# Another order for the first phase of a chunked attention and Mish feed-forward kernel

## The chip, the cores and the metric

The kernel runs on one core of a Trainium2 chip. The metric is the time of one execution on the device in microseconds (us); smaller is better. A core has five engines that run side by side and wait for each other through semaphores: TensorE (PE in the profile; PEld is its weight load), VectorE (DVE), ScalarE (ACT), GpSimd (POOL) and SyncE (SP, which here only issues DMA transfers). Each engine takes its instructions in the order in which they were written.

## The reference

Attention inside chunks of 64 tokens, then a feed-forward layer with Mish on its output:

```
scores = q_c @ k_c.T / sqrt(64)            # per batch, head and chunk of 64 tokens
attn = exp(scores - max); attn = attn / (sum(attn) + 1e-9)
x = (attn @ v_c)  -> 4608 tokens x 512
h = x @ w_in                               # 512 x 2048
g = h * tanh(softplus(h))                  # Mish
out = g @ w_out                            # 2048 x 512
```

All inputs are 32-bit floats, but for the two weights, which the kernel reads as pairs of 32-bit words and turns into 32-bit floats itself.

## The kernel before, in words

**Precision.** Each operand of the two large products is kept as a high part (rounded to the type of the fast matmul) and a low part (the rest). A product is three matmuls: low by high, high by high, high by low. `up` (line 282) does this for h = x W_in, 12 matmuls for a tile of 128 features and 512 tokens; `down` (L328) for the output.

**Weights.** There are 32 weight tiles of 128 x 512, 16 of W_in (i0 to i15) and 16 of W_out (o0 to o15), taken in the order i0, i1, i2, o0, i3, o1, i4, ... A tile goes through five steps. `load` (L82): one DMA of 512 KB. `scale` (L87): two ACT passes, L91 for the upper words (into a tile `wic` or `woc`) and L100 for the lower words (in place, in `wis` or `wos`; for i0 and i1 one byte each). `bits` (L105): two DVE passes, a shift (L110 or L113) and a merge with the sign (L114). `hi` (L121): an ACT copy into `wi_h` or `wo_h`. `lo` (L124): a DVE subtraction into `wi_l` or `wo_l`. All of it is done once, in the first ninth of the tokens' work.

**Attention.** Tokens come in pairs of 128-token tiles: 18 pairs, two to a block of 512 tokens. The steps of a pair are scores (PE, `s`), max and subtraction (DVE, `m`, `p`), exponential (ACT L220), sum, reciprocal and norm (DVE), transposes (PE, `pt`), a copy (ACT L251, `ps`), values (PE, `av`) and the split of x into `xh` (ACT L272) and `xl` (DVE L275).

**The first phase.** `prologue` (L383) does pairs 0 and 1, each as two halves (FIRST and SECOND, one tile each), between the first steps of the weight tiles i0, i1, i2, o0 and i3. `keep_busy` (L369) puts matmuls between that nobody reads (`spare`). The first `up`, on the columns A of pair 0, stands ahead of the transposes of pair 1, and the one on the columns B of pair 1 behind its values. After that come the slots (L452): in each, one `up`, one `down`, and the steps of two weight tiles as long as there are any.

**What sets the order.** Everything is written out by hand under `manual_schedule`: the order of the calls is the order of each engine's instructions. The pool of the raw weight tiles has four buffers, so a `load` waits on SP until the steps of an earlier tile are done. A new table of functions is loaded on ACT where the kind of function changes (`ACT_TABLE_LOAD`); the one at L417 is drawn by an activation of one column, `early`.

Of the kernel before, what the change touches and what calls it, by code (L numbers as in the profile page):

```python
# [18 lines left out]
P = 128  # L19
# [5 lines left out]
def kernel(  # L25
# [58 lines left out]
        nc.sync.dma_start(out=a.rearrange("p n t -> p (n t)"), in_=w32[m][f])  # L84
        wc[m, f] = {"a": a}

    def w_scale(m, f):  # L87
        d = wc[m, f]
        a = d["a"]
        d["c"] = c = wst.tile([P, DM], U32, name=f"w{m}c_{f}", tag="c")  # L90
        nc.scalar.activation(  # L91
            out=c.bitcast(F32), in_=a[:, :, 1].bitcast(F32), func=AF.Copy, scale=2.0**-112
        )
        low = a[:, :, 0]
        if bytewise(m, f):
            out = a.rearrange("p n t -> p (n t)").bitcast(U8)
            out = out.rearrange("p (n b) -> p n b", b=8)[:, :, 4]
        else:
            out = low.bitcast(I32)
        nc.scalar.activation(out=out, in_=low, func=AF.Copy, scale=7.499 / 2.0**32)  # L100

    def bytewise(m, f):
        return m == "i" and f < 2

    def w_bits(m, f):  # L105
        c, a = wc[m, f]["c"], wc[m, f]["a"]
        left, both, either = ALU.logical_shift_left, ALU.bitwise_and, ALU.bitwise_or
        sign = 0x80000000
        if bytewise(m, f):
            nc.vector.tensor_scalar(out=c, in0=c, scalar1=3, scalar2=None, op0=left)  # L110
            sign |= 7
        else:
            nc.vector.scalar_tensor_tensor(out=c, in0=c, scalar=3, in1=a[:, :, 0], op0=left, op1=either)  # L113
        nc.vector.scalar_tensor_tensor(out=c, in0=a[:, :, 1], scalar=sign, in1=c, op0=both, op1=either)  # L114

    def w_dst(m, f, part):
        if m == "o":
# [15 lines left out]
    for f in range(NF):  # L133
        order += [("i", f + 2)] if f + 2 < NF else []
        order += [("o", f)]
    steps = {"load": w_load, "scale": w_scale, "bits": w_bits, "hi": w_hi, "lo": w_lo}

    def w(step, n):
        if n < len(order):
            steps[step](*order[n])  # L140
# [143 lines left out]
    it = {}  # L284
    acc = {}

    def up(i, cols=slice(0, TOK), last="x"):

        b, f = divmod(i, NF)
        xh, xl = xts[b]  # L290
        if i not in it:
            it[i] = {"h": ps_h.tile([P, TOK], F32, name=f"h_{i}", tag="h")}
        h = it[i]["h"]
        n = 0
        parts = ((wi_l, xh), (wi_h, xh), (wi_h, xl))
        for w_, x in parts if last == "x" else reversed(parts):
            for kt in range(NK):
                nc.tensor.matmul(  # L298
                    h[:, cols],
                    lhsT=w_[:, f, kt],  # L300
                    rhs=x[:, kt, cols],
                    start=(n == 0),
                    stop=(n == 3 * NK - 1),
                )
                n += 1

    def mish(i):
        d = it[i]
# [66 lines left out]
    def prologue():  # L375

        A, B = slice(0, PTOK), slice(PTOK, TOK)
        O0, O2 = (ps_o, "o0"), (ps_o, "o2")
        room = xp.tile([P, 2, 2, H, CHUNK], F32, name="room_qk", tag="xh")
        room_v = xp.tile([P, 2, 2, H, CHUNK], F32, name="room_v", tag="xl")  # L380
        load_qk(0, None, (FIRST, SECOND), (nc.sync, nc.scalar))
        w("load", 0)
        load_v(0, room_v[:, 0])  # L383
        load_qk(1, (room[:, 0], room[:, 1]), (FIRST, SECOND))
        w("load", 1)
        load_v(1, room_v[:, 1])
        w("load", 2)
        w("load", 3)
        for t, place in (FIRST, HOME), (SECOND, O0):
            keep_busy(7 if t == FIRST else 3)  # L390
            a_scores(0, t, place)
            a_max(0, t)
            a_sub(0, t)
            a_exp(0, t)
        w("scale", 0)
        for t, place in (FIRST, O2), (SECOND, HOME):
            a_inverse(0, t)
            a_norm(0, t)
            keep_busy(9 if t == FIRST else 3)
            a_transpose(0, t, place)  # L400
            a_copy(0, t)
        w("bits", 0)
        w("hi", 0)
        w("lo", 0)
        for t, place in (FIRST, O0), (SECOND, O2):
            a_values(0, t, place)
        for t in FIRST, SECOND:
            a_hi(0, t)
            a_lo(0, t)
        w("scale", 1)  # L410
        for t, place in (FIRST, HOME), (SECOND, O0):
            a_scores(1, t, place)
            a_max(1, t)
            a_sub(1, t)
            a_exp(1, t)
        w("scale", 2)
        nc.scalar.activation(out=early, in_=ident[:, :1], func=AF.Mish)  # L417
        load_qk(2)
        w("load", 4)
        up(0, A)  # L420
        for t, place in (FIRST, O2), (SECOND, HOME):
            a_inverse(1, t)
            a_norm(1, t)
            keep_busy(8 if t == FIRST else 4)
            a_transpose(1, t, place)
            a_copy(1, t)
        w("bits", 1)
        w("hi", 1)
        w("bits", 2)
        for t, place in (FIRST, O0), (SECOND, O2):  # L430
            a_values(1, t, place)
        for t in FIRST, SECOND:
            a_hi(1, t)
            a_lo(1, t)
        w("hi", 2)
        w("scale", 3)
        w("load", 5)
        w("lo", 1)
        w("lo", 2)
        w("bits", 3)  # L440
        w("scale", 4)
        up(0, B)
        up(1, last="w")
        mish(0)
        w("load", 6)

# [10 lines left out]
    def slot(s):  # L457
        a = plan.get(s, {})
        n = 2 * s + 3

        if 1 <= s and s + 1 < N:
            up(s + 1, last="w")
        if "t" in a:
            a_transpose(a["t"])
        if "v" in a:
            a_values(a["v"])
        if "s" in a:
            a_scores(a["s"])
        if 1 <= s <= N:
            down(s - 1)  # L470

        w("load", n + 4)
        w("hi", n)
        if s < N:
            g_hi(s)
            g_lo(s)
        w("scale", n + 2)
        w("bits", n + 1)
        w("lo", n)
        if "max" in a:  # L480
            a_max(a["max"])
        if "norm" in a:
            a_norm(a["norm"])
        if "t" in a:
            a_copy(a["t"])
        if "exp" in a:
# [73 lines left out]
```

## Time and profile before

| | |
|---|---|
| Time, median of 3 runs | 877.64 us (875.27 to 877.67) |
| The profiled execution's own time | 876.71 us |
| Its span, first to last instruction | 874.9 us |
| PE busy | 860.4 us, 98% of the span |
| DVE busy | 341.5 us, 39% |
| ACT busy | 256.0 us, 29% |
| DMA queue of the transfers (q1) | 53.49 MB, 20.5% of 16 engines' span |

The span is cut into what each engine did. A share of busy time is a mean over the whole span: in the second to the fifth fortieth of it (22 to 109 us) the page shows DVE and ACT at 80% or more, while the weights are made, and both at 10 to 50% afterwards; PE is at 90% or more from the second fortieth to the last but one. The last instruction ends at 874.9 us; the run's own time is 1.8 us more.

### The profile page before, as it was taken

Reading aid. Unit: us, or ns where it says so; the run is one execution under the profiler, and the core shown is the slowest. Engines: PE = TensorE matmul, PEld = TensorE weight load, DVE = VectorE, ACT = ScalarE, POOL = GpSimd, SP = SyncE. Lnnn points to the kernel's source line nnn. Section 1 sums busy time; section 2 is a strip of 40 time slices with the busy share of each in tenths; the row PEclk is TensorE's granted clock in tenths of the full one; section 3 lists DMA queues with packets and bytes.
Section 4 is the critical chain, followed back from the end, with each engine's and each line's share of the span. In section 5 each row is a group of like instructions: output and inputs, shape, how many; then the busy total and the mean of one; then the engine's idle time right before and its main releaser. Section 6 shows DMA issues by size and latency. Waiting matters only on the chain.

```text
span 874.9 us, 13635 instructions
## 1 busy us (share of the span) xinstructions
PE 860.4 (98%) x5984; PEld 709.6 (81%) x5984; DVE 341.5 (39%) x533; ACT 256.0 (29%) x362; POOL 0.7 (0%) x6
## 2 busy tenths in 40 slices
PE   7999999999999999999999999999999999999997
PEld 6877788888888888888888888888888888888886
DVE  5889854242433233333424242423342342422221
ACT  5888832121312112221212131212212121311111
POOL 0000000000000000000000000000000000000000
PEclk9999999999999999999999999999999999999999
DMA  7557512101310130102110131013011202002001
GB/s 289 195 167 245 189 37 61 49 25 49 73 49 25 49 73 25 49 26 51 46 55 18 50 73 49 25 50 73 25 49 49 50 23 73 1 1 49 1 0 49
DMA packets 25179, 55.40 MB, mean 63 GB/s; under 512 B 2592, under 2 KB 2592, under 8 KB 25120
## 3 DMA queue, kind: packets, MB, share of 16 engines
q1 hardware_dynamic: 24512, 53.49, 20.5%
q8 instruction: 47, 0.77, 0.4%
q10 hardware_dynamic: 608, 1.05, 0.3%
q14 instruction: 12, 0.10, 0.0%
HBM read 45.09 MB, written 9.44 MB: 62 GB/s over the span
## 4 chain that ended last, share of the span: by engine, by line
PE 91%; DVE 4%; ACT 3%; issue 2%; ACTq 0%; POOLq 0%; POOL 0%
PE o_o L340 41%; PE h L298 41%; PE s L170 2%; PE av L170 2%; PE pt L241 2%; PE o_a L340 1%; PE spare L371 1%; DVE wo_l L125 1%; DVE wic L113 1%; DVE woc L114 1%; DVE wi_l L125 1%; DVE woc L113 0%; DVE m L197 0%; DVE xl L275 0%; ACT L310 0%
## 5 line engine op out<-in xcount | busy, mean ns | idle before, releaser
L318 DVE CAST gh<-z 128x512 fp32r<-128x512 f32 x136 | 57.8, 425 | 468.2 <-PE o_o L340 468.2
L340 PE MATMUL o_o<-wo_h,gl 128*128 128x512 f32 x560 | 222.9, 398 | 0.3 <-DVE gl L323 0.3
L340 PE MATMUL o_o<-wo_l,gh 128*128 128x512 f32 x560 | 218.4, 390 | 1.4 <-DVE wo_l L125 1.4
L340 PE MATMUL o_o<-wo_h,gh 128*128 128x512 f32 x560 | 218.3, 390 | 0.0
L310 ACT ACTIVATE z<-h 128x512 f32<-128x512 f32 x144 | 86.2, 599 | 450.7 <-PE h L298 344.7
L298 PE MATMUL h<-xh,wi_l 128*128 128x512 f32 (+1 forms) x580 | 154.9, 389 | 0.8 <-ACT xh L272 0.8
L298 PE MATMUL h<-xh,wi_h 128*128 128x512 f32 (+1 forms) x580 | 154.6, 388 | 0.0
L298 PE MATMUL h<-xl,wi_h 128*128 128x512 f32 (+1 forms) x580 | 154.6, 389 | 0.0
L298 PEld LDWEIGHTS h<-xh,wi_l 128*128 128x128 f32 x580 | 108.8, 189 | 23.3 <-ACT xh L272 0.9
L298 PEld LDWEIGHTS h<-xh,wi_h 128*128 128x128 f32 x580 | 108.9, 189 | 22.3
L298 PEld LDWEIGHTS h<-xl,wi_h 128*128 128x128 f32 x580 | 108.7, 189 | 22.2
L340 PEld LDWEIGHTS o_o<-wo_h,gl 128*128 128x128 f32 x560 | 105.1, 188 | 23.5 <-ACT z L310 0.7
L340 PEld LDWEIGHTS o_o<-wo_l,gh 128*128 128x128 f32 x560 | 105.2, 188 | 22.2 <-DVE wo_l L125 1.7
L340 PEld LDWEIGHTS o_o<-wo_h,gh 128*128 128x128 f32 x560 | 105.1, 188 | 22.1
L323 DVE TENSOR_TENSOR gl<-z,gh 128x512 fp32r<-128x512 f32 x144 | 99.7, 692 | 8.3 <-ACT gh L316 3.6
L251 ACT COPY ps<-pt 128x1024 f32<-128x1024 f32 (+1 forms) x20 | 18.6, 932 | 81.8 <-PE pt L241 81.8
L310 ACT ACT_TABLE_LOAD x16 | 20.5, 1283 | 34.5 <-PE h L298 34.5
L354 DVE COPY ob<-o_o 128x512 f32<-128x512 f32 x17 | 11.8, 692 | 35.2 <-ACT ob L356 32.8
L197 DVE TENSOR_REDUCE m<-s 128x16 f32<-128x1024 f32 (+1 forms) x20 | 22.2, 1112 | 7.5 <-PE s L170 7.4
L170 PEld LDWEIGHTS s<-k,q 64*64 64x64 f32 x1088 | 17.7, 135 | 6.4 <-issue 5.5
L211 DVE TENSOR_TENSOR p<-s,m 128x1024 f32<-128x1024 f32 (+1 forms) x20 | 22.3, 1117 | 0.6
L275 DVE TENSOR_TENSOR xl<-av,xh 128x1024 fp32r<-128x1024 f32 (+1 forms) x20 | 22.1, 1111 | 0.9 <-ACT xh L272 0.9
(48 smaller groups left out, 407.3 us busy)
## 6 DMA issues: line engine op xcount, KB each, us to landing
out<-ob SPq DMA_DIRECT2D x68, 128.0 KB, 2.4
wis<-in_w_in SPq DMA_DIRECT2D x16, 512.0 KB, 3.5
wos<-in_w_out SPq DMA_DIRECT2D x16, 512.0 KB, 3.8
q<-in_q SPq DMA_DIRECT2D x16, 512.0 KB, 3.7
k<-in_k SPq DMA_DIRECT2D x16, 512.0 KB, 3.7
v<-in_v SPq DMA_DIRECT2D x16, 512.0 KB, 4.0
room_v<-in_v SPq DMA_DIRECT2D x2, 512.0 KB, 7.3
q<-in_q SPq DMA_DIRECT2D x2, 256.0 KB, 3.9
```

Of the source, the lines that this page charges most:

```text
L125: nc.vector.tensor_tensor(out=w_dst(m, f, 1), in0=wc.pop((m, f))["c"].bitcast(F32), in1=w_dst(m, f, 0).bitcast(F32), op=ALU.subtract,)
L170: nc.tensor.matmul(o[h * CHUNK : (h + 1) * CHUNK, c, t - ts.start, g], lhsT=l[rows, t, 2 * g + h], rhs=r[rows, t, 2 * g + h], start=True, ...
L197: nc.vector.tensor_reduce(out=small(j, "m", t), in_=st[j]["s", t.start].rearrange("p c t g k -> p c (t g) k"), op=ALU.max, axis=AX.X,)
L211: nc.vector.tensor_tensor(out=d["p"][:, t].rearrange("p t g c k -> p c (t g) k"), in0=d["s", t.start].rearrange("p c t g k -> p c (t g) k" ...
L241: nc.tensor.transpose(out=d["pt", ts.start][:, t - ts.start, g], in_=d["p"][:, t, g].rearrange("p c k -> p (c k)"), identity=ident,)
L251: nc.scalar.copy(out=d["ps"][:, t].rearrange("p t h k -> p (t h k)"), in_=d["pt", t.start][:, : t.stop - t.start].rearrange("p t g n -> p ...
L275: nc.vector.tensor_tensor(out=x_view(j, 1, t), in0=flat(st[j]["av", t.start]), in1=x_view(j, 0, t).bitcast(F32), op=ALU.subtract,)
L298: nc.tensor.matmul(h[:, cols], lhsT=w_[:, f, kt], rhs=x[:, kt, cols], start=(n == 0), stop=(n == 3 * NK - 1),)
L310: nc.scalar.activation(out=d["z"], in_=d["h"], func=AF.Mish)
L318: nc.vector.tensor_copy(out=d["gh"], in_=d["z"])
L323: nc.vector.tensor_tensor(out=d["gl"], in0=d["z"], in1=d["gh"].bitcast(F32), op=ALU.subtract)
L340: nc.tensor.matmul(acc[t], lhsT=g[:, sl], rhs=w_[:, f], start=(f == 0 and n == 0), stop=(f == NF - 1 and n == 2),)
```

## The change

No arithmetic is changed, and no instruction added or taken away: every engine has as many rows as before. Four steps of the weights can now be called apart (`w_upper` and `w_lower` for `w_scale`, `w_shift` and `w_merge` for `w_bits`), and `prologue` calls them elsewhere. `up` takes its three groups of four matmuls by number: 0 is low x by high weights, 1 is high by high, 2 is high x by low weights.

```
-        w("hi", 0)
-        w("lo", 0)
+        w("shift", 1)
         for t, place in (FIRST, O0), (SECOND, O2):
             a_values(0, t, place)
         for t in FIRST, SECOND:
             a_hi(0, t)
             a_lo(0, t)
-        w("scale", 1)
+        w("hi", 0)
+        w("lower", 1)
...
-        w("scale", 2)
         nc.scalar.activation(out=early, in_=ident[:, :1], func=AF.Mish)
         load_qk(2)
-        w("load", 4)
-        up(0, A)
+        up(0, A, (0, 1))
...
             a_copy(1, t)
-        w("bits", 1)
-        w("hi", 1)
-        w("bits", 2)
+            if t == FIRST:
+                w("scale", 2)
+        w("lo", 0)
+        w("merge", 1)
+        w("load", 4)
+        w("shift", 2)
         for t, place in (FIRST, O0), (SECOND, O2):
             a_values(1, t, place)
         for t in FIRST, SECOND:
             a_hi(1, t)
             a_lo(1, t)
+        w("hi", 1)
+        w("merge", 2)
         w("hi", 2)
         w("scale", 3)
...
-        up(0, B)
-        up(1, last="w")
+        up(0, A, (2,))
+        up(0, B, (1, 2, 0), (1, 2, 0))
+        up(1)
         mish(0)
```

Besides, `w("upper", 1)` stands behind the copy of pair 0's first half. The slots keep their order.

First place: ACT, from the copies of pair 0's transposes (`ps<-pt`) to the exponentials of pair 1. `wic_170` is the scaled tile of i0, `wis_109` the raw tile of i1, `av` the values. Before:

```order
L251 COPY ps_192<-pt_0_187 128x512
L251 COPY ps_192<-pt_1_202 128x512
L122 CAST wi_h<-wic_170 128x512
L272 CAST xh_246<-av_0_212 128x2x4x64
L272 CAST xh_246<-av_1_229 128x2x4x64
L91 ACTIVATE wic_252<-wis_109 128x512
L100 ACTIVATE wis_109<-wis_109 128x512
L220 ACTIVATE p_274<-p_274 128x512 x2
```

After:

```order
L265 COPY ps_192<-pt_0_187 128x512
L90 ACTIVATE wic_194<-wis_109 128x512
L265 COPY ps_192<-pt_1_204 128x512
L286 CAST xh_247<-av_0_213 128x2x4x64
L286 CAST xh_247<-av_1_230 128x2x4x64
L135 CAST wi_h<-wic_170 128x512
L102 ACTIVATE wis_109<-wis_109 128x512
L234 ACTIVATE p_274<-p_274 128x512 x2
```

The upper words of i1 are scaled between the two copies, the two `xh` come ahead of the copy `wi_h` of i0, and the lower words of i1 stay behind them.

Second place: ACT, from the exponentials of pair 1 to the copy of i2 (`wis_112` raw, `wic_298` or `wic_332` scaled). Before:

```order
L91 ACTIVATE wic_298<-wis_112 128x512
L100 ACTIVATE wis_112<-wis_112 128x512
L417 ACT_TABLE_LOAD
L417 ACTIVATE early<-ident 128x1
L251 COPY ps_339<-pt_0_334 128x512
L251 COPY ps_339<-pt_1_350 128x512
L122 CAST wi_h<-wic_252 128x512
L272 CAST xh_246<-av_0_361 128x2x4x64
L272 CAST xh_246<-av_1_378 128x2x4x64
L122 CAST wi_h<-wic_298 128x512
```

After:

```order
L431 ACT_TABLE_LOAD
L431 ACTIVATE early<-ident 128x1
L265 COPY ps_330<-pt_0_325 128x512
L90 ACTIVATE wic_332<-wis_112 128x512
L102 ACTIVATE wis_112<-wis_112 128x512
L265 COPY ps_330<-pt_1_344 128x512
L286 CAST xh_247<-av_0_355 128x2x4x64
L286 CAST xh_247<-av_1_372 128x2x4x64
L135 CAST wi_h<-wic_194 128x512
L135 CAST wi_h<-wic_332 128x512
```

The table load now follows the exponentials; the two passes on i2 stand between the copies of the two halves, and both `wi_h` copies, of i1 and i2, stand behind both `xh`.

Third place: DVE, from the last norm of pair 1 to the first step of o0 (`woc`). Before:

```order
L232 TENSOR_TENSOR p_274<-p_274,r_1_341 128x2x4x64
L110 TENSOR_SCALAR wic_252<-wic_252 128x512
L114 SCALAR_TENSOR_TENSOR wic_252<-wis_109,wic_252 128x512
L113 SCALAR_TENSOR_TENSOR wic_298<-wic_298,wis_112 128x512
L114 SCALAR_TENSOR_TENSOR wic_298<-wis_112,wic_298 128x512
L275 TENSOR_TENSOR xl_247<-av_0_361,xh_246 128x2x4x64
L275 TENSOR_TENSOR xl_247<-av_1_378,xh_246 128x2x4x64
L125 TENSOR_TENSOR wi_l<-wic_252,wi_h 128x512
L125 TENSOR_TENSOR wi_l<-wic_298,wi_h 128x512
L113 SCALAR_TENSOR_TENSOR woc_400<-woc_400,wos_114 128x512
```

After:

```order
L246 TENSOR_TENSOR p_274<-p_274,r_1_335 128x2x4x64
L138 TENSOR_TENSOR wi_l<-wic_170,wi_h 128x512
L123 SCALAR_TENSOR_TENSOR wic_194<-wis_109,wic_194 128x512
L118 SCALAR_TENSOR_TENSOR wic_332<-wic_332,wis_112 128x512
L289 TENSOR_TENSOR xl_248<-av_0_355,xh_247 128x2x4x64
L289 TENSOR_TENSOR xl_248<-av_1_372,xh_247 128x2x4x64
L123 SCALAR_TENSOR_TENSOR wic_332<-wis_112,wic_332 128x512
L138 TENSOR_TENSOR wi_l<-wic_194,wi_h 128x512
L138 TENSOR_TENSOR wi_l<-wic_332,wi_h 128x512
L118 SCALAR_TENSOR_TENSOR woc_396<-woc_396,wos_114 128x512
```

The low part of i0 and the merge of i1 now come first, and the merge of i2, which the copy `wi_h` of i2 on ACT needs, moved from ahead of the two `xl` to behind them.

## Rows read from the trace of the kernel before

**Rows 1.** Waits of PE: waited for, us in total, times, longest.

```profile
PE o_o L340 <- DVE wo_l L125: 1.4, 1, 1.4
...
PE o_o L340 <- DVE gl L323: 0.3, 1, 0.3
```

**Rows 2.** Waits of PE from 60 us to the end, longest first.

```profile
PE s L170 <- PE h L298: 0.4, 1, 0.4
```

**Rows 3.** The chain that ended last, 24 to 60: start, us, what.

```profile
25.61 0.59 ACT ps L251
...
27.24 1.04 DVE xl L275 x2
...
31.09 0.62 ACT wo_h L122
...
32.26 0.69 DVE gl L323
...
48.76 0.61 ACT wi_h L122
...
54.72 2.77 PE o_o L340 x11
```

**Rows 4.** Timeline of ACT: start, us, instruction [idle before <-releaser].

```profile
12.80 0.59 ACT L251 COPY ps<-pt 128x512 f32<-128x512 f32 x1 [1.18 <-PE pt L241]
...
24.28 0.59 ACT L251 COPY ps<-pt 128x512 f32<-128x512 f32 x1 [0.51 <-PE pt L241]
...
26.61 1.08 ACT L272 CAST xh<-av 128x512 fp32r<-128x512 f32 x2
27.57 0.64 ACT L122 CAST wi_h<-wic 128x512 fp32r<-128x512 f32 x1
...
29.25 0.68 ACT L91 ACTIVATE wic<-wis 128x512 f32<-128x512 f32 x1
...
30.38 0.59 ACT L310 ACTIVATE z<-h 128x512 f32<-128x512 f32 x1
...
34.97 0.68 ACT L91 ACTIVATE wic<-wis 128x512 f32<-128x512 f32 x1
```

**Rows 5.** DMA issues from 5.5 to 5.6: KB, us to landing.

```profile
wis<-in_w_in SPq DMA_DIRECT2D x1, 512.0 KB, 7.1
```

**Rows 6.** Timeline of DVE.

```profile
14.55 1.28 DVE L275 TENSOR_TENSOR xl<-av,xh 128x512 fp32r<-128x512 f32 x2
...
21.53 0.69 DVE L232 TENSOR_TENSOR p<-p,r 128x512 f32<-128x512 f32 x1
...
25.69 0.69 DVE L114 SCALAR_TENSOR_TENSOR wic<-wis,wic 128x512 uint32<-128x512 uint32 x1
```

**Rows 7.** Timeline of PE.

```profile
15.29 0.34 PE L170 MATMUL s<-room_qk 64*64 64x64 f32 x8 [0.69 <-DVE xl L275]
18.32 0.67 PE L170 MATMUL s<-room_qk 64*64 64x64 f32 x24 [2.69 <-issue]
...
20.79 1.05 PE L298 MATMUL h<-xl,wi_h 128*128 128x256 f32 x4
21.65 2.16 PE L371 MATMUL spare<-ident 128*128 128x128 f32 x16
23.65 0.60 PE L241 MATMUL pt<-ident,p 128*128 128x128 f32 x4
...
25.51 1.44 PE L170 MATMUL av<-ps,room_v 64*64 64x64 f32 x64
```

**Rows 8.** DMA queues from 15.7 to 15.8: packets, MB, share.

```profile
q8 instruction: 1, 0.02, 67.6%
```

**Rows 9.** Windows: us; PE, PEld, DVE, ACT, POOL busy; PE clock; DMA.

```profile
15.00:18.70 3.70, 0.72 (x32) 0.59 (x32) 2.12 (x4) 2.41 (x3) 0.00 (x0) 1.00 0.93 350
18.70:22.10 3.40, 3.40 (x31) 3.28 (x21) 2.92 (x6) 1.61 (x3) 0.00 (x0) 0.50 0.04 12
50.00:55.00 5.00, 3.30 (x14) 2.24 (x13) 4.86 (x10) 3.52 (x7) 0.00 (x0) 1.00 0.18 75
```

More of the change, by code (lines that the diff above doesn't have):

```diff
@@ L85, in w_load, with w_upper @@
         wc[m, f] = {"a": a}
[L87 to L90, printed above, removed]
+    def w_upper(m, f):
+        a = wc[m, f]["a"]
+        wc[m, f]["c"] = c = wst.tile([P, DM], U32, name=f"w{m}c_{f}", tag="c")
         nc.scalar.activation(
@@ L93, in w_scale, with w_lower @@
         )
+    def w_lower(m, f):
+        a = wc[m, f]["a"]
         low = a[:, :, 0]
@@ L100, in w_scale, with w_shift, w_merge, w_bits @@
         nc.scalar.activation(out=out, in_=low, func=AF.Copy, scale=7.499 / 2.0**32)
+    def w_scale(m, f):
+        w_upper(m, f)
+        w_lower(m, f)
     def bytewise(m, f):
         return m == "i" and f < 2
-    def w_bits(m, f):
+    left, both, either = ALU.logical_shift_left, ALU.bitwise_and, ALU.bitwise_or
+    def w_shift(m, f):
         c, a = wc[m, f]["c"], wc[m, f]["a"]
-        left, both, either = ALU.logical_shift_left, ALU.bitwise_and, ALU.bitwise_or
-        sign = 0x80000000
         if bytewise(m, f):
             nc.vector.tensor_scalar(out=c, in0=c, scalar1=3, scalar2=None, op0=left)
-            sign |= 7
         else:
             nc.vector.scalar_tensor_tensor(out=c, in0=c, scalar=3, in1=a[:, :, 0], op0=left, op1=either)
-        nc.vector.scalar_tensor_tensor(out=c, in0=a[:, :, 1], scalar=sign, in1=c, op0=both, op1=either)
+    def w_merge(m, f):
+        c, a = wc[m, f]["c"], wc[m, f]["a"]
+        keep = 0x80000007 if bytewise(m, f) else 0x80000000
+        nc.vector.scalar_tensor_tensor(out=c, in0=a[:, :, 1], scalar=keep, in1=c, op0=both, op1=either)
+    def w_bits(m, f):
+        w_shift(m, f)
+        w_merge(m, f)
     def w_dst(m, f, part):
@@ L136 @@
     steps = {"load": w_load, "scale": w_scale, "bits": w_bits, "hi": w_hi, "lo": w_lo}
+    steps.update({"upper": w_upper, "lower": w_lower, "shift": w_shift, "merge": w_merge})
     def w(step, n):
@@ L285, with up @@
     acc = {}
-    def up(i, cols=slice(0, TOK), last="x"):
+    def up(i, cols=slice(0, TOK), which=(0, 1, 2), order_=(0, 1, 2)):
         b, f = divmod(i, NF)
@@ L293, in up @@
         h = it[i]["h"]
-        n = 0
-        parts = ((wi_l, xh), (wi_h, xh), (wi_h, xl))
-        for w_, x in parts if last == "x" else reversed(parts):
+        parts = ((wi_h, xl), (wi_h, xh), (wi_l, xh))
+        for n in which:
+            w_, x = parts[n]
             for kt in range(NK):
@@ L301, in up @@
                     rhs=x[:, kt, cols],
-                    start=(n == 0),
-                    stop=(n == 3 * NK - 1),
+                    start=(n == order_[0] and kt == 0),
+                    stop=(n == order_[-1] and kt == NK - 1),
                 )
-                n += 1
     def mish(i):
@@ L401, in prologue @@
             a_copy(0, t)
+            if t == FIRST:
+                w("upper", 1)
         w("bits", 0)
-        w("hi", 0)
-        w("lo", 0)
+        w("shift", 1)
         for t, place in (FIRST, O0), (SECOND, O2):
@@ L426, in prologue @@
             a_copy(1, t)
-        w("bits", 1)
-        w("hi", 1)
-        w("bits", 2)
+            if t == FIRST:
+                w("scale", 2)
[3 more added lines that the diff above has]
+        w("shift", 2)
         for t, place in (FIRST, O0), (SECOND, O2):
@@ L461, in slot @@
         if 1 <= s and s + 1 < N:
-            up(s + 1, last="w")
+            up(s + 1)
         if "t" in a:
```

## The prediction

> **What bounds the kernel now.** I read the busy times first: PE works in 98% of the span, so the time can only come from the few microseconds in which PE waits or runs at half clock. The waits of PE come second. In the early part there are two on the output product, 1.4 us for the low weights of o3 (the fourth tile of W_out) and 0.3 us for a `gl` [rows 1]; after 60 us no wait is longer than 0.4 us [rows 2], so from there on whatever PE has lost stays lost to the end. The third view is the chain that ended last, read backwards from that wait. PE's matmuls at 54.72 are released by DVE, DVE by ACT's `wi_h` at 48.76, and so on without a gap back to `gl` at 32.26, `wo_h` at 31.09, the two `xl` at 27.24 and the copy `ps` at 25.61 [rows 3]. From 25.6 to 54.7 us the end is set by DVE and ACT handing work to each other, not by PE. So I ask of each edit what it does to `gl` at 32.26. A microsecond there is a microsecond of the total, later or earlier, until PE's own slack of 1.4 + 0.3 = 1.7 us is used up on the early side [rows 1].
>
> **The change part by part.** No row is added or removed, so only orders and waits count. Durations that repeat: a split cast on ACT starts 0.48 us after the one before it (two from 26.61 to 27.57) and lasts 0.59; a pair of scale passes takes 1.13 (29.25 to 30.38) [rows 4]; a DVE pass over 512 columns lasts 0.69 [rows 6] and the next one starts about 0.6 later.
>
> *Upper words of i1 between the two copies of pair 0.* ACT must now wait there for the load of i1, issued in 5.5 to 5.6 and 7.1 us on its way [rows 5]: 12.6 to 12.7. The pass then holds ACT for 0.57 (half a pair), and the second copy starts at 13.27 instead of 12.80 [rows 4], 0.47 late; behind it on ACT are both `xh`.
>
> *x ahead of the weight copy.* That loss is more than made good for the first half: `wi_h` of i0 is no longer in between, the first `xh` runs from 13.75 to 14.34, and DVE, free of the low part of i0, makes the first `xl` from 14.36 to 15.05. It ran from 14.55 before [rows 6], to 15.24. The scores of pair 1's second half, which wait for it at 15.29 [rows 7], start 0.19 earlier. The second `xl` ends at 15.9 as before and stands beside those scores.
>
> *The stall.* After 8 of these 32 score matmuls PE stands for 2.69 us, and no instruction releases it [rows 7]; a packet of the instruction queue begins in the same tenth of a microsecond [rows 8]. I read it as PE waiting for its own instructions. The rows on PE ahead of that point are the same in both kernels, so I keep the stall at full length: the scores resume at 18.13 instead of 18.32. If it is tied to the transfers rather than to PE, they resume at 18.32, and 0.1 to 0.2 is lost again. The Trainium skill ("Runtime: NRT & Kernel Launch", Instruction fetch mechanics) calls the cost of crossing from one block of instructions to the next "mostly hidden"; the trace shows 2.69 us in the open. By the rule the stall would be chance and could be gone in the next kernel, which is rival A.
>
> *A third of the first `up` moved away, table load ahead.* The stall is followed by a stretch at half clock, 0.50 from 18.7 to 22.1 [rows 9], in which PE does `up` on the columns A, then the spare matmuls. The third group, 20.79 to 21.65, now goes behind the values. The spare ones start at 21.65 - 0.86 - 0.19 = 20.60. They took 2.00 (to 23.65), 0.45 of it at half clock: 1.78 at full clock. Now 1.50 at half clock does 0.75 of this, and the rest ends at 22.1 + 1.03 = 23.13. The first transposes start there, 0.52 early, since the norm that they need ends at 21.53 + 0.69 = 22.22 or before [rows 6]. ACT is free by then, with the scale passes of i2 gone from in front of it, and the copy follows 0.63 behind (23.65 to 24.28 before): 23.76.
>
> *Scale of i2 between the copies of pair 1.* The pair takes its 1.13 in between: 23.76 + 0.48 + 1.13 = 25.37 for the second copy, though PE's transposes would allow 25.61 - 0.52 = 25.09. The hole between the copies (24.28 to 25.61) covered the pair only in part, because its second pass must end first: 0.28 of the 0.52 is lost. The copy is 0.24 early.
>
> *Merge of i2 behind both `xl`.* This is the term that decides. The values ended at 25.51 + 1.44 = 26.95, 0.75 after the copy's end; now 25.37 + 0.59 + 0.75 = 26.71. The second `xh` runs 26.73 to 27.32, the second `xl` 27.34 to 28.03, and the merge 27.94 to 28.63. Before, it was done at 25.69 + 0.69 = 26.38 [rows 6], and ACT's copy of i2 followed the `xh` without a pause at 27.57 [rows 4]. Now ACT, having copied i1, waits for the merge until 28.65: 1.08 late. Behind it on ACT, in order, are the scales of o0 and i3, `z`, `wo_h` and `gh`. From that copy to `z` is 2.81 (27.57 to 30.38), so `z` starts at 31.46 and `wo_h` at 31.97. Before, `wo_h` waited some 0.2 for DVE (0.5 after `z` would have been 30.9, it started at 31.09); DVE's two passes on o0 end at about 31.8 now and no longer hold it. So `wo_h` is 0.88 late, and `gl` with it, 33.14 for 32.26. That goes to the end.
>
> *At no cost.* The low part of i0, the merge of i1 and the shift of i2 fill DVE between the last norm and the first `xl`; without that cover, each would cost 0.6. The moved third of `up` fills PE while it waits for `xh`; uncovered, it is four matmuls, 0.5. SP's order of loads is the same. The load of i4 waits for the merge of i2, so it is issued 2.2 later, at 28.7; with the 7.1 us of the crowded start [rows 5] it lands at 35.8, and its reader, at 34.97 before [rows 4], comes at 34.97 + 0.9 = 35.9. Nothing is lost as long as it takes no longer.
>
> *Sum.* +0.9 us. On the profiled execution's own time, 876.71, that is 877.6. It lies 0.93 below the median of the runs shown, 877.64, from which the sum is 878.5. I take the middle, **878.0 us**.
>
> *Bounds.* What I can't read is where the half clock falls. At full clock all through, the norm sets the transposes (22.05), the second copy comes at 24.3, and the sum is 0.9 - 1.1 = -0.2: 876.5. At half clock until the transposes, the spare ones take 3.56 and end at 24.16: +1.9, 878.6. The landing of i1's load is worth nothing if it comes 0.5 earlier (the upper words would then wait for nothing) and 1 us for each us later. I take the trace's values, being the only ones it shows, and keep 876.5 to 879 for the range.
>
> **The rivals.**
>
> *A. The stall is hidden.* For it: the rule above. Against it: the same rows on PE, and DMA as crowded as before. The clock would not fall, and the norm alone would set the transposes. DVE, running from the first `xl` through five passes at 0.6, would end its second subtraction near 18.4 instead of 20.3, so the norm ends at 22.03 - 1.9 = 20.1, 3.0 ahead of 23.13, and all behind it follows: 0.9 - 3.0 = -2.1, **874.6**.
>
> *B. Full clock on the spare matmuls,* the bound above: **876.5**. For it: the fastest run shown, 875.27, is 1.4 below the profiled one, which some runs without the half clock would explain. Against it: PE was busy 0.72 of 3.70 us ahead of the fall [rows 9], and that is not changed.
>
> *C. x alone decides.* The change does what its order says, x comes 0.5 earlier (second `xl` done at 28.03 for 28.53), and `z` follows x, not the merge: 876.71 - 0.5 = **876.2**. For it: PE starts on the columns B earlier. Against it: ACT's order, where `z` stands behind the copy of i2.
>
> *D. The longer wait costs the clock.* Place: PE at 46 to 55 us. There it waited 1.7 us; now it arrives 0.4 earlier and is released 0.9 later, so it waits 3.0. From 50 to 55 PE was busy 3.30 of 5.00 and kept its clock, while the 0.72 of 3.70 ahead of 18.7 were followed by 3.4 us at 0.50 [rows 9]. If the pieces of the wait fall close enough for the same, 3.4 us at half clock lose 1.7: 877.6 + 1.7 = **879.3**, slower than before by 2.6. It decides once the wait nears the 2.69 us of the stall in one piece; so far I see it in three (about 0.6, 0.9 and 1.4).
>
> **How the numbers follow.** Forecast 0.55 (its own range 876.8 to 879.2), A 0.05, B 0.15, C 0.13, D 0.12. About 0.3%, 2.6 us, is what a measurement of this kernel can tell from no change; the three runs alone lie 2.4 apart. The forecast, B and C lie within it; A comes near it from below and D stands on its edge, or past it from the higher median. With the scatter of the runs: faster 0.06, same 0.82, slower 0.12. The range goes from 875.7, which leaves out A, to 880.0, which takes in D from the profiled time.
>
> **What would show it.** Right: ACT idle for some 0.8 us ahead of the copy `wi_h` of i2, released by DVE's merge; `z` of the first tile near 31.4; `gl` near 33.1; PE's waits between 46 and 56 us near 3 us in all; the transposes of pair 1 some 0.5 earlier; the 2.7 us stall in the same scores. Wrong: a copy of i2 that starts before 28; a first `up` that ends and is followed by `z` before 30.4; PE's wait for the low part of o3 gone or shorter; no half clock near 19 us.

## The result, and the profile after

The changed kernel takes 877.15 us (median of 22 runs, 876.05 to 880.54), the kernel before 875.40 us (22 runs beside them, 874.48 to 877.76). The ratio is 1.0022, 95% interval 1.0015 to 1.0029: 1.9 us slower (1.3 to 2.5), which is within 0.3%. The ratio is an estimate of its own and not the quotient of the two medians, here and in the table below. The forecast was 878.0 us, +0.9 us by its sum. The profiled execution of the changed kernel took 878.03 us with a span of 876.2 us and a mean clock of 0.995; before it was 876.71 us, 874.9 us and 0.998.

PE's waits come first, as before; the columns are us in total, times, and the longest.

```profile
PE o_o L353 <- DVE wo_l L138: 1.9, 2, 1.4
...
PE s L184 <- issue: 1.3, 1, 1.3
PE o_o L353 <- DVE gl L336: 0.4, 1, 0.4
```

The wait for the low weights has grown from 1.4 to 1.9 us and comes in two pieces (0.50 at o2, which is new, and 1.36 at o3, where it was 1.37), and the one for `gl` from 0.3 to 0.4 [rows 1]. The wait without a releaser in the scores has shrunk from 2.69 [rows 7] to 1.3. So one loss is bigger and one smaller, and the question is which of the two belongs to the change.

The chain that ended last shows where the order bites (start, us, what):

```profile
25.42 0.74 PE av L184 x32
...
26.18 0.60 ACT xh L286
...
26.80 0.69 DVE xl L289
27.49 0.61 DVE wic L123
28.12 0.02 ACT wi_h L135
...
31.00 0.47 ACT z L323
...
32.53 0.69 DVE gl L336
...
54.23 0.70 DVE wo_l L138
...
54.97 4.38 PE o_o L353 x11
```

Now a pass of DVE on the weights, the merge of i2 (L123), stands in the chain between `xl` and `wi_h`, and from there to `gl` it is ACT's queue. Before, the chain stayed on DVE behind the two `xl`, through this row and the two passes on o0, and reached ACT only at `wo_h` [rows 3]:

```profile
28.44 1.28 DVE wi_l L125 x2
```

The last row of the chain after is a second difference: the same eleven matmuls take 4.38 us and took 2.77 [rows 3].

The timeline of ACT, then one row of DVE (start, us, instruction, idle time before it and its releaser):

```profile
13.29 0.69 ACT L90 ACTIVATE wic<-wis 128x512 f32<-128x512 f32 x1 [0.56 <-DMA wis<-in_w_in]
13.90 0.59 ACT L265 COPY ps<-pt 128x512 f32<-128x512 f32 x1
...
28.12 0.62 ACT L135 CAST wi_h<-wic 128x512 fp32r<-128x512 f32 x1 [0.84 <-DVE wic L123]
...
30.88 0.58 ACT L323 ACTIVATE z<-h 128x512 f32<-128x512 f32 x1
...
27.41 0.68 DVE L123 SCALAR_TENSOR_TENSOR wic<-wis,wic 128x512 uint32<-128x512 uint32 x1
```

ACT stands idle for 0.84 us ahead of the copy of i2, which it took without a pause before [rows 4], and the releaser is the merge that ran at 25.69 before [rows 6]. Measured from the end of pair 1's values, `gl` came 32.26 - 26.95 = 5.3 us later before [rows 3, 7]; now it comes 32.53 - (25.42 + 0.69) = 6.4 later (the values' row is in PE's timeline below). I call this distance C: it holds the merge, and nothing of what happens earlier. From `gl` to the low weights of o3 both kernels take 22.4 us. From there to the end of the span every profile of this document takes 820.3 us (820.26 to 820.34), except those of the changed kernel and of E5, which take 821.3. So what a profile loses, it loses ahead of these low weights or right behind them.

The timeline of PE in the two places in question:

```profile
13.24 0.63 PE L255 MATMUL pt<-ident,p 128*128 128x128 f32 x4 [0.47 <-DVE p L246]
...
15.93 0.34 PE L184 MATMUL s<-room_qk 64*64 64x64 f32 x8 [0.22 <-DVE xl L289]
17.58 0.79 PE L184 MATMUL s<-room_qk 64*64 64x64 f32 x24 [1.31 <-issue]
...
22.44 0.60 PE L255 MATMUL pt<-ident,p 128*128 128x128 f32 x4
...
25.42 0.69 PE L184 MATMUL av<-ps,room_v 64*64 64x64 f32 x32 [0.42 <-ACT ps L265]
...
53.13 0.47 PE L353 MATMUL o_o<-wo_h,gl 128*128 128x512 f32 x1 [0.43 <-DVE gl L336]
54.97 0.51 PE L353 MATMUL o_o<-wo_l,gh 128*128 128x512 f32 x1 [1.36 <-DVE wo_l L138]
55.30 0.60 PE L353 MATMUL o_o<-wo_h,gh 128*128 128x512 f32 x1
55.70 0.63 PE L353 MATMUL o_o<-wo_h,gl 128*128 128x512 f32 x1
```

The stall sits behind the same 8 score matmuls as before, but lasts 1.31 us. The transposes of pair 1 start at 22.44 for 23.65 [rows 7]. At o3 a matmul that takes 0.40 at full clock takes 0.60 to 0.63 right behind the wait. The windows confirm it (us; busy time of PE, PEld, DVE, ACT, POOL; PE clock; DMA share and GB/s):

```profile
15.00:18.70 3.70, 2.17 (x83) 1.78 (x75) 2.95 (x5) 3.11 (x5) 0.00 (x0) 0.88 0.92 350
18.70:22.10 3.40, 3.40 (x21) 3.40 (x21) 3.26 (x7) 2.12 (x3) 0.00 (x0) 0.63 0.08 29
50.00:55.00 5.00, 3.20 (x14) 2.09 (x12) 4.86 (x10) 3.52 (x8) 0.00 (x0) 1.00 0.24 93
55.00:60.00 5.00, 5.00 (x15) 3.96 (x16) 4.33 (x7) 3.79 (x7) 0.00 (x0) 0.66 0.71 188
```

There are two stretches at half clock (1.2 GHz), one behind the stall, as before [rows 9], and one behind the wait at o3. The profile of before does not have the second:

```profile
55.00:60.00 5.00, 5.00 (x23) 4.09 (x23) 4.33 (x7) 3.69 (x7) 0.00 (x0) 1.00 0.69 200
```

The runs' mean clocks say how often: 10 of the 22 runs of the changed kernel are at 0.996 or below (median 878.66), 9 at 0.997 or 0.998 (877.14) and 3 at 0.999 or above (876.15). One stretch of 3.4 us at half clock is 0.5 × 3.4 / 876 = 0.002 of the mean clock, so these are runs with about two such stretches in all, one and none. The mean does not say where they lie: E1's profile below, at 0.995, has two without a gap, from 17.7 to 24.6 us. Of 105 runs of the kernel before, beside the experiments, 5 are in the lowest group, 77 in the middle and 23 at 0.999 or above.

The instruction queue has its packet (packets, MB, share) in the window 14.9 to 15.0, where it was at 15.7 before [rows 8]:

```profile
q8 instruction: 1, 0.02, 67.9%
```

### The profile page after: what moved, and what is told of

It reads as the page before. It is cut to its first block, busy times and chain, and to the rows that moved or that the text cites. A ratio compares the mean times of both kernels' runs of the same rounds, so it can differ in the third digit from the quotient of the medians.

```text
span 876.2 us, 13638 instructions
## 1 busy us (share of the span) xinstructions
PE 863.8 (99%) x5984; PEld 711.5 (81%) x5984; DVE 341.8 (39%) x533; ACT 256.4 (29%) x362; POOL 0.7 (0%) x6
## 4 chain that ended last, share of the span: by engine, by line
PE 93%; ACT 3%; DVE 3%; issue 1%; ACTq 0%; POOLq 0%; POOL 0%
PE o_o L353 43%; PE h L312 42%; PE s L184 2%; PE av L184 2%; PE pt L255 2%; PE o_a L353 1%; PE spare L384 1%; DVE wo_l L138 0%; DVE wic L118 0%; DVE m L211 0%; ACT woc L90 0%; ACT wos L102 0%; ACT L323 0%; ACT L234 0%; DVE p L246 0%
## 5 line engine op out<-in xcount | busy, mean ns | idle before, releaser
L312 PEld LDWEIGHTS h<-xh,wi_l 128*128 128x128 f32 x580 | 108.4, 188 | 22.4
```

The source lines that it names most:

```text
L312: nc.tensor.matmul(h[:, cols], lhsT=w_[:, f, kt], rhs=x[:, kt, cols], start=(n == order_[0] and kt == 0), stop=(n == order_[-1] and kt == ...
```

## The experiments

The theory: the late merge delays `gl` by about 1.1 us from the values on, and the longer waits up to o3 now and then cost the clock. The rivals: the whole front (x first, the scale passes of i1 that wait for their load) is what costs; or the instruction stall moved and did it. The runs came in three groups, E1 to E4, E5 to E8 and E9 to E12, each beside 35 runs of the kernel before (medians 875.31, 875.16 and 875.16), and each group on another chip, so that rows of one group compare best. The table has the median, the ratio to before with its 95% interval, how many runs had a mean clock of 0.999 or more, and from the one profiled execution C and the end of the low weights of o3 (54.66 in the profile of before).

| | median us | ratio | at 0.999 | C | o3 low done |
|---|---|---|---|---|---|
| changed kernel | 877.15 | 1.0022 [1.0015, 1.0029] | 3 of 22 | 6.42 | 54.92 |
| E1 changed, merge early | 876.50 | 1.0008 [0.9998, 1.0018] | 0 of 12 | 5.50 | 56.52 |
| E2 before, merge late | 875.65 | 1.0001 [0.9991, 1.0011] | 10 of 12 | 6.63 | 53.21 |
| E3 changed, low weights last | 876.21 | 1.0008 [0.9998, 1.0017] | 7 of 12 | 6.42 | 53.85 |
| E4 before, low weights last | 874.59 | 0.9990 [0.9979, 1.0002] | 8 of 11 | 5.32 | 51.75 |
| E5 before, wide spares | 875.81 | 1.0007 [0.9998, 1.0015] | 2 of 11 | 5.32 | 52.09 |
| E6 E1 with wide spares | 875.49 | 0.9999 [0.9991, 1.0008] | 1 of 11 | 5.50 | 53.27 |
| E7 changed, wait filled | 876.47 | 1.0013 [1.0004, 1.0022] | 9 of 12 | 6.42 | 54.31 |
| E8 E6, scale of i3 later | 874.56 | 0.9988 [0.9980, 0.9997] | 5 of 11 | 4.19 | 52.90 |
| E9 before, wait filled | 874.40 | 0.9986 [0.9978, 0.9995] | 9 of 11 | 5.32 | 52.68 |
| E10 before, wide and filled | 875.23 | 0.9999 [0.9990, 1.0007] | 4 of 12 | 5.31 | 53.14 |
| E11 changed, wide and filled | 876.43 | 1.0007 [0.9998, 1.0015] | 5 of 11 | 6.43 | 54.23 |
| E12 E8 with wait filled | 874.37 | 0.9987 [0.9979, 0.9996] | 6 of 11 | 4.20 | 51.53 |

### The merge alone: E1 and E2

E1 is the changed kernel with the merge of i2 back ahead of the values; E2 is the kernel before with only the merge moved behind `xl`.

```diff
 E1, changed kernel
-        w("shift", 2)
+        w("bits", 2)
...
-        w("merge", 2)
 E2, kernel before
-        w("bits", 2)
+        w("shift", 2)
...
+        w("merge", 2)
```

> The changed kernel with one move undone: DVE's merge of i2 stands right behind its shift again, ahead of both xl of pair 1. Theory 1 (the copy wi_h of i2 on ACT waits for that merge, and z, wo_h, gh and gl queue behind it): ACT's 0.84 us of waiting ahead of that copy is gone, the copy starts about 27.1 instead of 28.12 when the values end as in the changed kernel's profile, gl starts 0.8 to 1.1 us earlier against the end of the second xh, PE's wait for the low part of o3 shrinks by as much, and the time falls by 0.8 to 2.7 us against the changed kernel (the more, the oftener that kernel falls to half clock near 55 us). Rival 1 (the order of the first half of the prologue, or the table load, cost the time): the median falls by less than 0.4 us. Rival 2 (PE is set by something behind 60 us): no change.

> The kernel before with this one move done alone: DVE's merge of i2 behind both xl of pair 1; all else, the table load and the two passes on i2 included, is as before. Theory 1: the second xl ends about 0.6 us sooner (27.9), the merge at 28.5, the copy wi_h of i2 starts near 28.5 instead of 27.57, gl near 33.0 instead of 32.26, and the time rises by 0.6 to 1.0 us at equal clock, more in runs that fall to half clock near 55 us. Rival 1: within 0.4 us of the kernel before.

In E1 the idle time between the copies `wi_h` of i1 and i2 is gone (timeline of ACT, then of PE):

```profile
29.16 1.14 ACT L135 CAST wi_h<-wic 128x512 fp32r<-128x512 f32 x2
...
19.20 0.92 PE L184 MATMUL s<-room_qk 64*64 64x64 f32 x24 [2.87 <-issue]
```

In E2 it is there (ACT, DVE, PE):

```profile
26.40 0.62 ACT L129 CAST wi_h<-wic 128x512 fp32r<-128x512 f32 x1 [1.47 <-DVE wic L117]
...
30.81 0.69 DVE L331 TENSOR_TENSOR gl<-z,gh 128x512 fp32r<-128x512 f32 x1 [1.21 <-ACT gh L324]
...
15.32 0.69 PE L178 MATMUL s<-room_qk 64*64 64x64 f32 x32 [0.69 <-DVE xl L283]
```

C follows the merge in both directions: 6.42 to 5.50 when it goes back, 5.32 to 6.63 when it alone goes late. That settles the mechanism. The medians do not settle its size. E1's is 0.65 below that of the changed kernel, less than the 0.8 to 2.7 expected, and its profiled execution is the slowest of its runs, with a stall of 2.87 us and half clock from 17.7 to 24.6. E2's interval includes no change, +0.34 us in the median: its profile has no stall at all, and 10 of its 12 runs are at 0.999 or above against 8 of 35 for its kernel before. At that clock E2's 10 runs have a median of 875.53 and the 8 of the kernel before 874.84: 0.69 more, as expected (0.6 to 1.0). What the late merge costs E2, the clock gives back. Why E2 keeps its clock is not settled: its profile shows waits as long as the changed kernel's, 0.42 us for `gl` and 0.5 and 1.37 for low weights, and full clock behind them.

### The wait at o3: E3 and E4

In both kernels, in the output tiles 1 to 14 of the first block, the products with the low weights go behind the other two of all four token tiles, so that they are asked for some 1.8 us later.

```diff
+        if 1 <= i < NF - 1:
+            for g, w_ in (d["gl"], wo_h), (d["gh"], wo_h), (d["gh"], wo_l):
+                for t in ts:
+                    nc.tensor.matmul(...)
```

> The changed kernel, but the output product of the feature tiles 1 to 14 of the first block takes its groups in another order: low x high for all four token tiles, then high x high, then high x low weights, so that the low weights are asked for 1.8 us later. It takes away PE's wait for wo_l without making DVE any faster. Theory 2 (that wait, with the one for gl, brings the half clock near 55 us in part of the runs): no wait of 1.4 us for o3, granted clock 1.00 from 50 to 60 us in the profile, the runs at 878 and above disappear, and the median falls by 1.3 (the wait alone) to 3 us against the changed kernel. Rival (the half clock there comes by chance, or the chain gives the wait back in a later tile): the median falls by less than 0.5 us, and waits of PE for wo_l or gl turn up at o4 or later.

> The kernel before with the same order of the output product. Theory 2: the wait of 1.4 us goes here too, with no half clock to win: 1.0 to 1.4 us faster than the kernel before, and faster than the changed kernel with that order by what the first phase costs at full clock, 0.3 to 0.9 us. Rival: same as the kernel before within 0.4 us.

PE in E3:

```profile
48.61 1.20 PE L312 MATMUL h<-xl,wi_h 128*128 128x512 f32 x4 [0.75 <-ACT wi_h L135]
...
52.06 1.17 PE L365 MATMUL o_o<-wo_h,gl 128*128 128x512 f32 x4 [0.43 <-DVE gl L336]
...
78.32 1.16 PE L184 MATMUL s<-k,q 64*64 64x64 f32 x64 [1.59 <-DVE xl L289]
```

The wait for the low weights is gone and others stand in its place, 0.75 us for a `wi_h` and 1.59 us for the next pair's `xl` at 78 us; E4 has a wait of 1.6 us at the same scores, which shows no releaser. From the end of the low weights of o3 both take the 820.3 us of the others: in E3 PE waits for ACT and DVE at other places instead, while for E4 no row names what it waits for. At full clock E3 (876.04, 7 runs) stands where the changed kernel does (876.15, 3 runs). The medians fall by 0.9 (E3, from the changed kernel) and 0.7 us (E4, from before), and the runs that keep the clock are the more: 7 of 12 for 3 of 22, and 8 of 11 for 8 of 35. E4's interval reaches to no change. Both falls lie between what the theory (1.3 to 3, and 1.0 to 1.4) and its rival (less than 0.5, and 0.4) had. Between E3 and E4, which are of one group, the change costs 1.6 us (medians 876.21 and 874.59, at full clock 876.04 and 874.39), more than the 0.3 to 0.9 expected.

### The stall: E5 and E6

The spare matmuls that keep PE busy are issued four at a time as one matmul of 512 columns, in the kernel before (E5) and in E1 (E6). PE then has 60 instructions fewer ahead of the scores of pair 1's second half.

```diff
-            nc.tensor.matmul(spare["o"][:, :P], lhsT=ident, rhs=ident, ...)
+            nc.tensor.matmul(spare["o"][:, : k * P].rearrange(...), lhsT=ident,
+                rhs=ident.unsqueeze(1).broadcast_to([P, k, P]), ...)
```

> The kernel before, with the spare matmuls of keep_busy issued as wider ones: the same columns and the same time on PE, but 7 matmuls instead of 22 ahead of the scores of pair 1, so 60 instructions of PE fewer (each spare matmul is two weight loads and two matmuls in the profile). Theory 3 (the stall of PE sits at a fixed number of PE's instructions, where the next block of them has not arrived): it moves behind the second half's scores, 60 instructions on, into the first up or the spare matmuls, where it holds nothing up; from the start of those scores to the end of pair 1's values it is 8.9 us in every profile, as in the two profiles without a stall, instead of 11.66; the runs at 877 to 878 of the kernel before disappear, and its median falls by 0.2 to 1.0 us. Rival (the stall comes at a time, with the transfers, or is a chance of the run): it stays in those scores in some runs, and the median is within 0.2 us.

> The changed kernel with the merge of i2 ahead of both xl again, and with the wide spare matmuls. If the merge was the only part of the change that costs, and the stall is out of the way, what is left of the change (the scores of pair 1 start 0.45 us sooner against the first phase's start, from the end of the values to gl 5.5 us instead of 5.3) makes it 0.1 to 0.4 us faster than the kernel before with wide spare matmuls. Rival (the front half of the change costs by itself): slower than that kernel by more than 0.2 us.

PE in E5, in the first `up` and at o3:

```profile
15.50 0.69 PE L170 MATMUL s<-room_qk 64*64 64x64 f32 x32 [0.68 <-DVE xl L275]
...
18.49 0.50 PE L298 MATMUL h<-xh,wi_h 128*128 128x256 f32 x2 [1.39 <-issue]
...
52.14 0.50 PE L340 MATMUL o_o<-wo_l,gh 128*128 128x512 f32 x1 [1.37 <-DVE wo_l L125]
...
53.53 0.63 PE L340 MATMUL o_o<-wo_h,gl 128*128 128x512 f32 x1
```

And E5's windows:

```profile
18.50:22.00 3.50, 3.50 (x16) 2.15 (x16) 3.29 (x9) 3.25 (x6) 0.00 (x0) 1.00 0.02 7
...
53.30:56.70 3.40, 3.40 (x10) 2.63 (x9) 2.76 (x5) 2.17 (x5) 0.00 (x0) 0.51 0.57 184
```

The stall has moved from the scores into `up`. Counted from the program's start, 220 matmuls are recorded ahead of it in E5, in the changed kernel and in before alike: it sits at a count of PE's instructions, not at a place of the program. This E5 execution shows more: a kernel with the weight order of before, with no half clock behind the stall, has one behind the wait at o3, which was 1.37 us as in the profile of before [rows 1]. So the clock is at stake at o3 before the change as well. E5 is not faster for the better place of its stall, against the 0.2 to 1.0 us expected; 9 of its 11 runs have at least one stretch. Why its median is 0.6 us above before's stays open. E6's median is 0.3 below E5's, as expected, but the intervals overlap.

### The wait filled: E7 and E9

Six spare matmuls (twelve rows of the profile) go in behind the first matmul of o3, into the bank of a later `h`, so that PE is busy while it waits. E7 is the changed kernel, E9 the kernel before.

```diff
+                if i == 3 and t == 0 and n == 0:
+                    it[i + 3] = {"h": ps_h.tile(...)}
+                    for _ in range(6):
+                        nc.tensor.matmul(it[i + 3]["h"][:, :P], lhsT=ident, rhs=ident, ...)
```

> The changed kernel with six spare matmuls (1.3 us) put into PE's wait for the low part of o3, behind the first matmul of that tile's output product. The wait is not shortened, PE is only kept busy in it. Theory 2 (the half clock near 55 us comes from that wait): granted clock 1.00 from 50 to 60 us in the profile, no runs at 878 and above from that cause, the fastest runs as in the changed kernel (876.0 to 876.3), and the median 0.5 to 1.2 us below it. Rival (the slowest runs come from the stall and the half clock near 20 us alone): the same spread as the changed kernel, with about a third of the runs at 878 or more.

> The kernel before with the same six spare matmuls in PE's wait for the low part of o3. Most of its runs show a mean granted clock of 0.997 or 0.998, one stretch of half clock, and the profile of the kernel before with spare matmuls made wide had that stretch at 53.3 to 56.7 us, behind that wait. If the wait costs the kernel before its clock too, in most runs: most runs at 0.999 or 1.00 now, median 0.3 to 1.0 us below the kernel before. Rival (the half clock there is new with the change): same median and clocks as the kernel before.

PE in E7, and its window behind the wait:

```profile
52.83 1.50 PE L363 MATMUL h<-ident 128*128 128x128 f32 x12
54.36 0.50 PE L353 MATMUL o_o<-wo_l,gh 128*128 128x512 f32 x1
54.70 0.39 PE L353 MATMUL o_o<-wo_h,gh 128*128 128x512 f32 x1
```

```profile
55.00:60.00 5.00, 5.00 (x25) 4.11 (x24) 4.32 (x8) 3.35 (x7) 0.00 (x0) 1.00 0.60 203
```

The low weights of o3 come as long behind the values as in the changed kernel (C 6.42, then 22.4 us), and the clock stays at 1.00. In E7 9 of 12 runs keep 0.999 (3 of 22 without the filling), and the median falls by 0.7 us; the lowest run stays at 876.0, and two runs, of 878.26 and 878.88, are still at 0.996. In E9 it is 9 of 11 (8 of 35), 0.76 us below before. In the profiles the filling buys clock and nothing else, and by the runs it buys it in both kernels.

With the wait filled in both, E7 and E9 differ by 2.07 us, and the lowest run of E7 (876.00) is above the highest of E9 (875.00). So the change costs about 2 us here, in two kernels of different groups, that the clock at o3 has no part in. In the two profiles 1.1 of it is C, and another 0.5 is in front. Of that, 0.27 is there already at the transposes of pair 0's second half (13.22 against 12.95), ahead of everything that the change moves; the rest comes between them and the end of pair 1's values (12.26 against 12.01), where ACT waits 1.18 us for the load of i1 in E7. The last 0.4 of the medians' difference these two profiles don't show.

### The change with stall and wait out of the way: E10 and E11

Both kernels have the wide spare matmuls and the filled wait, each as above.

> The kernel before with the wide spare matmuls and the filled wait: neither the stall in the scores nor the half clock at o3 is left, so that what remains of the kernel before stands by itself. Expected 874.0 to 875.0 us with a spread under 1 us, and 8.87 us from pair 1's second scores to the end of its values, 5.3 from there to gl.

> The changed kernel with the wide spare matmuls and the filled wait, to be set against the run above. By the sum of the change's own terms (scores 0.2 to 0.45 sooner, from the end of the values to gl 6.42 us for 5.32) it is 0.6 to 0.9 us slower than that run. Rival (the first phase of the change costs by itself, or the merge's place is worth what the time moved in all): 1.3 us or more slower.

E10, the kernel before (ACT, DVE):

```profile
26.04 0.64 ACT L122 CAST wi_h<-wic 128x512 fp32r<-128x512 f32 x1
...
30.74 0.69 DVE L323 TENSOR_TENSOR gl<-z,gh 128x512 fp32r<-128x512 f32 x1 [1.21 <-ACT gh L316]
```

E11, the changed kernel:

```profile
12.49 0.69 ACT L90 ACTIVATE wic<-wis 128x512 f32<-128x512 f32 x1 [1.07 <-DMA wis<-in_w_in]
...
27.40 0.62 ACT L135 CAST wi_h<-wic 128x512 fp32r<-128x512 f32 x1 [0.83 <-DVE wic L123]
...
31.83 0.69 DVE L336 TENSOR_TENSOR gl<-z,gh 128x512 fp32r<-128x512 f32 x1 [1.21 <-ACT gh L329]
```

E10 missed what was expected, 874.0 to 875.0 with a spread under 1 us: it is at 875.23 with a spread of 2.1, and half clock still follows the stall, now in `up`. But the two profiles have it at the same place (18.0 to 21.4 and 17.9 to 21.3) and differ in little but the order. The low weights of o3 are done 54.23 - 53.14 = 1.09 later, C is 1.12 longer, the scores start 0.08 earlier and pair 1 takes 0.05 more. The medians differ by 1.20 us, the runs at full clock by 0.89 (875.79 of 5 and 874.90 of 4). The intervals of the two ratios overlap, so the size is good to some tenths only. In the profiles the late merge alone explains the difference. The medians' 1.20 lies between what was expected (0.6 to 0.9) and the rival (1.3 or more).

### A better order: E8 and E12

If ACT's queue up to `gh` sets the end, the two scale passes of i3, which stand there ahead of `z`, belong behind it. E8 is E6 with that; E12 is E8 with the filled wait.

```diff
-        w("scale", 4)
...
         mish(0)
+        g_hi(0)
+        w("scale", 4)
```

> As the run before last (merge of i2 early, wide spare matmuls), and ACT does the two scale passes of i3 behind z and gh of the first feature tile instead of ahead of them. If the order of ACT from the end of the values to gl sets the end, gl comes 1.6 us sooner (3.9 us behind the values' end instead of 5.5), the next step of DVE, the shift of i3, 1.1 us sooner, and the time falls by 1.0 to 1.2 us against that run. Rival (DVE's whole work up to 78 us sets the end, not where its chain starts): less than 0.4 us.

> The fastest kernel so far (changed kernel, merge of i2 early, wide spare matmuls, scale of i3 behind gh) with the filled wait. Its runs fell in two groups, 873.6 to 874.2 at clock 0.999 and 874.6 to 875.1 at 0.997; if the second is the half clock at o3, all runs lie near the first: median 873.6 to 874.0, 1.2 to 1.6 us faster than the kernel before. Rival: the median stays at 874.5.

E8's ACT and DVE:

```profile
28.67 0.59 ACT L323 ACTIVATE z<-h 128x512 f32<-128x512 f32 x1
29.29 0.62 ACT L329 CAST gh<-z 128x512 fp32r<-128x512 f32 x1
...
30.13 0.69 DVE L336 TENSOR_TENSOR gl<-z,gh 128x512 fp32r<-128x512 f32 x1
```

C falls from 5.50 to 4.19: the two passes are 1.1 us, and `gh` now follows `z` with no `wo_h` in between. From `gl` to the low weights of o3 it takes 22.77 us for 22.41, so that 0.95 of the 1.31 is left. The median falls by 0.93 us from E6 to E8 (1.0 to 1.2 expected), and E8 is faster than before by 0.12% (0.03 to 0.20%). That is the same lever as the late merge, pulled the other way. Filling the wait adds no more to it that could be seen: E12 is at 874.37, where 873.6 to 874.0 were expected, and 6 of its 11 runs keep 0.999 for 5 of 11 in E8. E8, E9 and E12 are 0.6 to 0.8 us below the kernel before, with intervals that leave out no change, and can't be told from each other.

## Why the prediction was right, and where it was not

**The deciding term was right in place and size.** The forecast put 33.14 - 26.71 = 6.43 us between the values and `gl`; it was 6.42. ACT's idle time of "some 0.8 us", released by the merge, was 0.84. E1 and E2 show that it is the merge, at 0.9 and 1.3 us of C; with the merge back E1 keeps 5.50 for the 5.32 of before, so up to 0.2 belongs to other moves. The whole change makes 1.12 between E10 and E11.

**Everything ahead of it came 0.6 us earlier than forecast,** `gl` at 32.53 for 33.14. The step that failed is "I keep the stall at full length". The other case that the step names, a stall tied to the transfers, is nearer to what the runs show, though not its figure: the scores resumed at 17.58, and it had 18.32. In all ten profiles with a stall PE resumed 2.4 to 2.7 us behind the start of the instruction packet: packets at 14.84 (E3), 14.98 (changed kernel), 15.74 (before) and 16.82 (E1), scores at 17.29, 17.58, 18.32 and 19.20. In E2, E4, E7 and E9 the packet came between 10.1 and 11.4 us, and there was no stall. That the packet holds PE's own instructions is inferred from these times; no row says whose they are. The Trainium skill ("Runtime: NRT & Kernel Launch", Instruction fetch mechanics) calls the cost of crossing from one block of instructions to the next "mostly hidden". The trace agrees for those four, and for the others it shows 1.3 to 2.9 us in the open; rival A, given 0.05, is what some executions do, with either order (E7 and E9).

**The load of i1 cost what the forecast had, where ACT waited for it as long.** The forecast let the first copy of pair 0 end at 11.63 (the copy before ran at 11.04 for 0.59) and the load land at 12.7, a wait of 1.07 us, and the scores gained 0.19. In E11 ACT waits those 1.07 us. Counted from the transposes of pair 0's second half, the scores of pair 1's second half start 0.16 sooner in E11 than in E10, and 0.07 sooner in E7 (a wait of 1.18) than in E9. In the changed kernel's own profile these transposes come at 13.24, where before had them at 12.14:

```profile
12.14 0.63 PE L241 MATMUL pt<-ident,p 128*128 128x128 f32 x4 [0.47 <-DVE p L232]
```

The load landed at 13.29, ACT waited 0.56, and from the transposes to the scores it took 15.93 - 13.24 = 2.69 us for 15.29 - 12.14 = 3.15. So there x first brought 0.46, and the front's late start, 1.1 us, took more than that away.

**Rival D was misread, and came true in part.** The forecast saw half clock behind the wait at o3 as something that only the change would bring, at 0.12, because the profile of before showed a clock of 1.00 there [rows 9]. That was one execution. E5 shows the same half clock in a kernel with before's order, and 82 of 105 runs of the kernel before have at least one stretch somewhere. The changed kernel's runs show two more often, 10 of 22 for 5 of 105. That the longer wait is the reason is not shown: at o3 itself PE waits 1.79 us for 1.70, the rest is at o2, and E2, with waits as long and 10 of 12 runs at full clock, speaks against it. Behind the wait it costs 4.38 - 2.77 = 1.6 us in the chain, as D's price of 1.7 had it; by the span's end 1.06 of it is left, since a later wait of 0.35 us, at the scores of 79 us, is gone, and smaller ones with it. No wait at o3 reached the stall's 2.69 us in one piece: pieces of 0.43 and 1.36 came ahead of the fall in the changed kernel, 0.34 and 1.37 in E5, and 0.33 and 1.37 in the profile of before and 0.42 and 1.37 in E2 were followed by full clock. The total of 2.3 us between 46 and 56 us was less than the 3.0 forecast: PE came to o2 0.9 us earlier than before (0.4 in the forecast), but the low weights of o3 came only 0.26 later (0.9), and PE's rows between the waits took some 0.5 longer.

**The sum.** The profiles add up as 0.26 us at the low weights of o3 (0.64 by which the scores of pair 1's second half start later, less 1.47 from there to the end of its values, where the stall was shorter, plus 1.10 in C) and 1.06 behind them from the clock, 1.3 in the spans. The ratio says 1.9. Against +0.9 the forecast lacked the clock, and its +0.9 at `gl` was 0.27 in the profile, by the luck of a short stall. Its time of 878.0 lies within 1 us of the result partly since two errors cancel: it started from between 876.71 and 877.64, and 22 runs put the kernel before at 875.40.

**What stays open:** why the filled pair differs by 2.07 us and the wide, filled pair by 1.20, of which C explains 1.1 in each; the time of E2; and the median of E5. One rival no run tests. In the four profiles of the changed order with narrow spare matmuls (changed kernel, E1, E3, E7) the transposes of pair 0's second half come at 12.96 to 13.31 us, in the four of before's order (before, E2, E4, E9) at 12.01 to 12.95, and with wide ones, in either order, at 11.86 to 12.70. Nothing that the change moves runs ahead of them, but four profiles a side do not show that it is chance, and it would count in the 2.07 and the 1.6 of E3 and E4.

## What to carry to other kernels

A pass that seems to lie in idle time of its engine is not free when another engine's queue, which keeps its order, has an instruction that waits for it ahead of critical work: follow what the waiting instruction holds back, as here `wi_h` held back `z`. Where a profile shows a wait of a microsecond or two on PE, look at the mean clocks of many runs before you call it free, since one execution shows the clock's fall or doesn't; a few spare matmuls in the wait kept the clock in 18 of the 23 runs of E7 and E9. A wait of PE that nothing in the profile ends and that sits at the same count of instructions in two kernels is not the order's doing, and its length in one profile is no base for a sum.

## What was not expected of the hardware

- The stall of PE that no instruction releases stands at a fixed count of its instructions: 219 or 220 recorded matmuls from the start in all ten profiles that have it. Its end goes with the packet, not with PE's arrival: none with packets up to 11.4 us, 1.3 to 2.9 us with packets from 14.8 to 16.8.
- PE's first rise to full clock comes at another time in each execution: the trace's record of the granted clock starts between 4.3 and 7.5 us (the windows print 1.00 ahead of it, for want of a record). The rows agree: six rows of spare matmuls take 0.94 us from 5.41 in the profile of before, whose record starts at 5.0, and 1.65 us from 5.70 in the changed kernel's, at 7.5. There the transposes of pair 0's second half come 1.1 us later, with the same instructions ahead of them.
